# Three kinds of ScalarE work placed later in a planned order: a long convolution beside a feed-forward block

## The chip, the cores and the metric

The kernel runs on one core of one Trainium2 chip. The metric is the device time of one execution in microseconds, as the median of several runs. The core has five engines, each with a queue of its own that it works off in order: TensorE (PE in the profile) for matmuls, VectorE (DVE), ScalarE (ACT), GpSimd (POOL) and SyncE (SP). SP and POOL issue the transfers (DMAs) here. Engines wait for one another by semaphores.

## The reference

`x` has 2048 rows of 1024 columns. Two branches work on its layer norm, and their sum is added to `x`.

```
xn = layernorm(x)
k_shift = sum over 4 taps of k shifted by 0..3 rows, times shift_k      # short causal convolution
kv = k_shift * v
y  = irfft(rfft(kv padded to 4096) * rfft(ssm_k padded to 4096))[:2048] # long causal convolution
A  = xn * (y + kv * ssm_D)
B  = silu(xn @ w1) @ w2                                                # 1024 -> 3584 -> 1024
out = x + A + B
```

All inputs and the output are float32.

## The kernel before

**Two branches side by side.** The feed-forward part is two large matrix products (GEMM1 with `w1`, GEMM2 with `w2`) in fp16. Each float32 operand is split into a high part (ScalarE, a scaled copy) and a low part (VectorE, the remainder), and a product takes three matmuls: high by high, high by low, low by high. Most of it runs as Strassen products, seven (P1 to P7) in place of eight. Results leave PSUM by ScalarE copies and silus and by VectorE sums (`evacuate`, `silu`, `evacuate2`, `result`); there are four PSUM banks for it, the ring `ff`. Lines L980 to L982 are the three matmuls of GEMM1, L1123 to L1125 those of GEMM2.

The convolution works on eight groups of 128 channels (`g` from 0 to 7). For each group, `gate` makes the signal `acc` (the taps and the product with `v`, in the tile `sig`). `signal_parts` splits it into high and low parts and turns it, `stage1` transforms it by matmuls (L1625 to L1627, tile `ps`), and `to_spec`, `forward`, `product` and `inverse` do the rest of the transform on VectorE in the tile `spec`. `result_parts` splits the result (`zh`, `zl`), `stage1_inv` transforms it back (L1813 to L1815, tile `py`), and `gated` multiplies it by rows of `x` (tile `xg`, some in `ht`) and sends it to the output.

**The order of the work is planned when the program is built.** Every operation is an `Op` with an engine, an estimated duration and a `margin`. The generators above are streams that yield operations, and wait for flags and free buffers. `Order.prepare` reckons when the operands of a stream's next operation are there, by the planner's own clock, and adds the margin; for a transfer the clock assumes a fixed latency and 345 GB a second (in `Order.run`). `Order.run` then always takes the operation that could start first, less a small bias of its stream, puts it at the end of its engine's queue, and goes on. The chip works off each queue in exactly that order, however long its transfers really take. The usual margin of a ScalarE or VectorE operation is 0.15 us.

**The three places that the change touches.**

- *Squares of w2* (`squares_w2`, `square_w2`). The norm of `w2` is needed before `w2` can be split. 28 loads of 512 KB go in turn to two buffers, `wraw` and `w2n`; ScalarE squares each in place with a running total, and this frees the buffer for the next load. After the last one, `norms_w2` makes the scales (among them a small matmul, `py<-q,one`), and then loads `w2` a second time through the same two buffers to split it for GEMM2 (`x<-wraw,tau` and `x<-w2n,tau`). The stream's bias is 0.01, nearly the lowest.
- *Rows of x for the gate* (`norm_rows`, bias 0). For each group and each of four `t`, two transfers of 128 KB fill a tile of `xg` (four buffers; some tiles come from `ht`), and four ScalarE operations subtract the mean. A tile's successor in the stream is loaded after that. The tile is free again when `gated` has sent it out.
- *Parts of the conv signal* (`signal_parts`, first called for group 0 through TensorE, for the groups from 1 on through DMA). For each of four `t`, `split` writes the high and low part of a quarter of `acc` into the single buffer `cm`; two transposing DMAs (`X`, SP queue) carry them back into `acc` turned. The next quarter needs the buffer, and so the end of these DMAs.

In the profile nearly all ScalarE operations have line L362, those of VectorE L351 and L354, and transfers from SP L338, its transposing ones L344, since helpers issue them; they are told apart by the tiles they write and read.

Of the kernel before, what the change touches and what calls it, by code (L numbers as in the profile page):

```python
# [15 lines left out]
AF = mybir.ActivationFunctionType  # L16
# [103 lines left out]
class Order:  # L120
# [27 lines left out]
    def add(self, gen, bias, floor=0.0):  # L148
        s = Stream(gen, bias, floor)
        self.streams.append(s)  # L150
        self.advance(s)
# [151 lines left out]
def h3_ffn_kernel(ctx, tc, x, kp, vs, fs, shift, dskip, w1, w2, cfwd, cinv, out):  # L303
# [26 lines left out]
    def A(f, o, ins, us=None, m=0.15):  # L330
        return Op("ACT", us or 1.02 * (0.16 + size(o) * 0.84e-3), 0.2, f, ins, [o], m)

    def T(f, o, ins, us, m=0.1):
        return Op("PE", us, 0.3, f, ins, [o], m)

    def L(o, i, m=0.3):
        n = size(o) * o.shape[0] * mybir.dt.size(o.dtype)
        return Op("SP", 0.4, 0.1, lambda: nc.sync.dma_start(o, i), [i], [o], m, n)  # L338

    def X(o, i, m=0.3, k=None):  # L340

        n = size(o) * o.shape[0] * mybir.dt.size(o.dtype)
        k = k or (1.2 if i.space == bass.MemoryType.DRAM else 3.0)
        return Op("SP", 0.65 + n / 240e3, 0.1, lambda: nc.sync.dma_start(o, i, transpose=True), [i], [o], m, k * n)  # L344
# [8 lines left out]
    def v_stt(o, a, s, b, op0, op1, **k):  # L353
        return V(lambda: nc.vector.scalar_tensor_tensor(o, a, s, b, op0=op0, op1=op1), o,  # L354
                 [a, b] + ([] if isinstance(s, float) else [s]), **k)

    def a_act(o, i, func, scale=1.0, bias=None, total=None):
        def f():
            kw = {} if bias is None else {"bias": bias}
            if total is not None:  # L360
                kw["accum_out"] = total
            nc.scalar.activation(o, i, func, scale=scale, **kw)  # L362
        ins = [i] + [s for s in (scale, bias) if s is not None and not isinstance(s, float)]
        p = A(f, o, ins)
        p.table = func if func in (AF.Silu, AF.Sqrt) else None
        p.busy += 0.07 * (len(ins) - 1) - 0.06 * (i.space == bass.MemoryType.PSUM)
        if total is not None:
            p.busy += 0.19
            p.writes.append(total)
        return p  # L370

    def split(hi, lo, src, scale, after=()):

        yield a_act(hi, src, AF.Copy, scale)
        yield v_stt(lo, src, scale, hi, MUL, SUB)
        for t in after:
            t.set()
# [11 lines left out]
    mu = cst.tile([P, NT], F32, name="mu")  # L389
# [57 lines left out]
    def norm(ring, ss, ns, then, flags, margin=1.5):  # L447
# [27 lines left out]
        for t in flags[1]:  # L475
            t.set()


    def small(o, i, scale, ins=()):

        return Op("ACT", 0.2, 0.2, lambda: nc.scalar.activation(o, i, AF.Copy, scale=scale), [i, *ins], [o], 0.15)
# [110 lines left out]
    def turned(src, tok, name, i, bias):  # L592

        yield ft.ready
        pt, ptok = ft.tile([P, KH, P])

        def mm():
            for c in range(KH):
                nc.tensor.transpose(pt[:, c, :], src[:, c * P:(c + 1) * P], ident)
        yield T(mm, pt, [src], 0.44, m=0.3)  # L600
        flag["turned", name, i].set()
        if tok is not None:
            tok.set()
        o = factor(name)[:, i]
        after = (ptok, flag["x", 0, name]) + ((flag["rows", i],) if name in ("A11", "A12") else ())
        add(split(o[:, :, 0], o[:, :, 1], pt, XS, after), bias)
# [27 lines left out]
    def shipped(names, i, src, toks):  # L634

        def steps():
            yield xst_r.ready if len(names) == 1 else xst_r.pairs
            rows, rtok = (xst_r.tile if len(names) == 1 else xst_r.pair)([P, len(names) * KH, 2, P], F16, len(names))
            yield from split(rows[:, :, 0], rows[:, :, 1], src.rearrange("p (k w) -> p k w", w=P), XS, toks)
            for n, name in enumerate(names):  # L640
                add(across(name, i, rows[:, n * KH:(n + 1) * KH], rtok), URGENT.get(name, 0.1))
        add(steps(), URGENT.get(names[0], 0.1))
# [665 lines left out]
    def squares_w2():  # L1308

        yield lambda: "wraw" in ctxs  # L1310
        yield flag["unit", SQ]
        rings = ctxs["wraw"], ctxs["w2n"]
        for i in range(NP):
            for h in range(2):
                yield lambda: any(r.pairs() for r in rings)
                raw, tok = next(r for r in rings if r.pairs()).pair([P, 2, W])
                yield L(raw, w2r[:, 2 * i:2 * i + 2, h * W:(h + 1) * W])
                add(square_w2(raw, tok, ss2[:, i, h:h + 1]), 0.01)
# [1 line left out]
    flag["w2 squares"] = Token(2 * NP)  # L1320

    def square_w2(raw, tok, o):
        yield a_act(raw, raw, AF.Square, total=o)
        tok.set()
        flag["w2 squares"].set()

# [132 lines left out]
    def convolution(floor):  # L1459
# [9 lines left out]
        acc = sig[:, 0]  # L1469
# [17 lines left out]
        def rest(floor):  # L1487

            yield flag["w done"]
            yield flag["w spilled"]  # L1490
            early_w.close()
            rb = late_w.enter_context(tc.tile_pool(name="rb", bufs=1, side="right"))
            for name, bufs in (("zh", 2), ("zl", 2), ("xg", XGB)):
                more[name] = ring(name, bufs, rb)
            ctxs["wraw"] = Halves(order, rb, "wraw", 1)
            for gen, bias in ((result_parts(), CB), (stage1_inv(), 0.02), (norm_rows(), 0.0), (norms_w2(), 0.03)):
                add(gen, bias, max(order.free["DVE"], order.free["ACT"]))
# [68 lines left out]
        def signal_parts():  # L1566

            for g in range(NG):
                yield flag["scales", g]
                kf, ktok = kfs[g]  # L1570
                sc, _ = scs[g]
                whole = [kparts[:, :, q].rearrange("p b t w -> p b (t w)") for q in range(2)]
                add(split(*whole, kf.rearrange("p b t w -> p b (t w)"), sc[:, 1:2], (ktok, flag["kparts", g])), CB)
                for t in TO:
                    there = acc16.rearrange("p b (i t) w -> p (b i) t w", i=2)[:, :, t]
                    two = [there[:, :, q * P:(q + 1) * P] for q in range(2)]
                    if g < BY_DMA:
                        yield py_r.ready
                        px, ptok = py_r.tile([P, 2, 2, P])

                        def mm():
                            for b in range(2):
                                for i in range(2):
                                    nc.tensor.transpose(px[:, b, i, :], acc[:, b, t + 4 * i, :], ident)
                        yield T(mm, px, [acc[:, :, t::4, :]], 0.44, m=2.0)
                        add(split(*two, px.rearrange("p b i w -> p (b i) w"), sc[:, 0:1], (ptok, flag["part", g, t])), CB)
                        continue
                    yield cm_r.ready
                    cm, ctok = cm_r.tile([P, 2, 2, 2, P], F16, 2)
                    yield from split(cm[:, 0], cm[:, 1], acc[:, :, t::4, :], sc[:, 0:1])  # L1590
                    flag["part", g, t].n = 2
                    for q, o in enumerate(two):
                        yield X(o, cm[:, q].rearrange("p b i w -> p (b i w)"))
                        ctok.set()
                        flag["part", g, t].set()
# [188 lines left out]
        def norm_rows():  # L1784

            for g in range(NG):
                for t in TO:
                    r = more["xg"]
                    yield lambda: r.ready() or flag["quads", 1]() and hts.ready()
                    xgs[g, t] = xg, _ = (r if r.ready() else hts).tile([P, 2, 2, P], uses=2)  # L1790
                    for b in range(2):
                        yield L(xg[:, b], x4[b][:, :, t, g * P:(g + 1) * P])
                    for b in range(2):
                        for i in range(2):
                            n = b * T2 + 4 * i + t
                            yield a_act(xg[:, b, i], xg[:, b, i], AF.Identity, -1.0, mu[:, n:n + 1])
                    flag["xg", g, t].set()

        def stage1_inv():
# [48 lines left out]
        for gen, bias in ((loads(), 0.05), (load_v(), 0.04), (gate(), 0.04), (signal_parts(), CB), (stage1(), 0.02),  # L1848
                          (transforms(), 0.02), (squares_w2(), 0.0), (rest(floor), 0.0)):
            add(gen, bias, floor)  # L1850
# [113 lines left out]
```

## Time and profile before

| | us |
|---|---|
| median of 3 runs | 1244.58 (1244.14 to 1245.72) |
| the profiled execution, its own time | 1244.12 |
| its span, first to last instruction | 1242.0 |
| first and last GEMM1 matmul | 15.6, 578.2 |
| first and last GEMM2 matmul | 579.7, 1238.1 |

The busy share of the engines in 40 slices of 31 us, in tenths (9 is 90% or more):

```profile
PE   9999999999999999999999999999999999999998
...
DVE  7999996996999779998899799899989979997981
ACT  7868997886688897559752732753363374554351
...
DMA  9598989899799899879986558489576784888776
```

A row of a view of waits names the engine that waited, what it waited for, and the microseconds in total, the number of times and the longest. In a timeline each row has a start, a duration, the engine, the line, the operation, and the output, an arrow and the inputs; a bracket gives the idle time just ahead and who ended it. The end of a matmul is modelled, so consecutive ones overlap in the records.

### The profile page before, as it was taken

How to read it: one execution, taken by the hardware profiler on the slowest of the kernel's cores; microseconds unless marked ns; L12 is line 12 of the kernel's file. 1: busy time of each engine (PE TensorE's matmuls, PEld its weight loads, DVE VectorE, ACT ScalarE, POOL GpSimd, SP SyncE). 2: the span in 40 equal slices, each digit the busy share in tenths (PEclk: the TensorE clock that was granted, in tenths of full speed). 3: DMA queues.
4: the chain of work that ended last, by engine and by line, in shares of the span. 5: the costliest groups of instructions: out<-in, count | busy, mean ns of one | idle time of the engine just before them, and what ended most of it. 6: DMA issues, size and time to landing. Idle time of an engine off the chain costs nothing.

```text
span 1242.0 us, 16865 instructions
## 1 busy us (share of the span) xinstructions
PE 1227.1 (99%) x6044; PEld 596.2 (48%) x6044; DVE 1107.2 (89%) x1248; ACT 775.7 (62%) x1357; POOL 83.3 (7%) x93
## 2 busy tenths in 40 slices
PE   9999999999999999999999999999999999999998
PEld 8544444444444544445444544544444454444454
DVE  7999996996999779998899799899989979997981
ACT  7868997886688897559752732753363374554351
POOL 0000000000000000000000000001030130123123
PEclk9999999999999999999999999999999999999999
DMA  9598989899799899879986558489576784888776
GB/s 369 127 315 265 322 301 325 262 258 217 233 346 291 241 309 295 244 205 315 297 269 153 155 186 171 122 293 278 125 168 169 178 170 141 180 150 133 164 142 97
DMA packets 277700, 278.77 MB, mean 224 GB/s; under 512 B 85616, under 2 KB 204656, under 8 KB 276336
## 3 DMA queue, kind: packets, MB, share of 16 engines
q1 hardware_dynamic: 261888, 261.17, 70.2%
q0 software_dynamic: 15728, 16.52, 10.3%
q8 instruction: 47, 0.77, 0.3%
q14 instruction: 37, 0.30, 0.1%
HBM read 171.46 MB, written 88.34 MB: 209 GB/s over the span
## 4 chain that ended last, share of the span: by engine, by line
PE 70%; DVE 19%; DMA 4%; issue 3%; ACT 2%; SPq 0%; DVEq 0%; ACTq 0%
PE ff L980 10%; PE ff L981 10%; PE ff L982 10%; PE ff L1123 10%; PE ff L1124 10%; PE ff L1125 10%; DVE spec L351 7%; DVE tmp L351 2%; DVE wo L354 2%; DVE sig L354 1%; PE ps L1625 1%; PE ps L1627 1%; PE ps L1626 1%; DMA wraw<-in_w 1%; DVE x L354 1%
## 5 line engine op out<-in xcount | busy, mean ns | idle before, releaser
L1123 PE MATMUL ff<-x,wo 128*128 128x512 f16 x868 | 328.1, 378 | 2.0 <-ACT hf L362 0.9
L1125 PE MATMUL ff<-x,wo 128*128 128x512 f16 x868 | 328.1, 378 | 0.0
L1124 PE MATMUL ff<-x,wo 128*128 128x512 f16 x868 | 328.1, 378 | 0.0
L980 PE MATMUL ff<-x,wo 128*128 128x512 f16 (+1 forms) x808 | 302.8, 375 | 3.3 <-ACT hf L362 3.3
L982 PE MATMUL ff<-x,wo 128*128 128x512 f16 (+1 forms) x808 | 302.8, 375 | 0.0
L981 PE MATMUL ff<-x,wo 128*128 128x512 f16 (+1 forms) x808 | 302.8, 375 | 0.0
L351 DVE TENSOR_TENSOR spec<-spec 128x1024 f32<-128x1024 f32 (+2 forms) x232 | 259.3, 1146 | 2.0
L1125 PEld LDWEIGHTS <-wo 128*128 128x128 f16 x868 | 84.9, 98 | 101.6
L1124 PEld LDWEIGHTS <-wo 128*128 128x128 f16 x868 | 84.9, 98 | 101.3 <-issue 3.3
L1123 PEld LDWEIGHTS <-wo 128*128 128x128 f16 x868 | 85.8, 99 | 98.6
L982 PEld LDWEIGHTS <-wo 128*128 128x128 f16 x808 | 79.0, 98 | 92.4 <-DVE wo L354 0.5
L981 PEld LDWEIGHTS <-wo 128*128 128x128 f16 x808 | 79.0, 98 | 92.0 <-issue 3.9
L980 PEld LDWEIGHTS <-wo 128*128 128x128 f16 x808 | 80.5, 100 | 88.1
L351 DVE TENSOR_TENSOR tmp<-spec 128x2048 f32<-128x2048 f32 (+1 forms) x48 | 92.5, 1934 | 1.0
L354 DVE SCALAR_TENSOR_TENSOR ht<-hf,wsc,ht 128x1024 f16<-128x1024 f32 (+1 forms) x56 | 67.2, 1203 | 19.6 <-ACT ht L362 19.6
L362 ACT ACTIVATE spec<-spec 128x1024 bf16<-128x1024 f32 x32 | 33.7, 1053 | 59.6 <-DVE spec L351 59.5
L354 DVE SCALAR_TENSOR_TENSOR wo<-raw,wsc,wo 128x1024 f16<-128x1024 f32 (+1 forms) x56 | 63.9, 1147 | 4.4 <-ACT wo L362 4.0
L362 ACT ACTIVATE wo<-raw,wsc 128x1024 f16<-128x1024 f32 (+1 forms) x56 | 57.7, 1033 | 11.7 <-DVE raw L351 8.8
L354 DVE SCALAR_TENSOR_TENSOR sig<-kin,taps,sig 128x1024 f32<-128x1024 f32 x48 | 61.5, 1281 | 2.5 <-ACT sig L362 2.4
L348 POOL DMA_DIRECT2D out<-hf x44 | 39.3, 906 | 342.7 <-ACT hf L362 280.4
L351 DVE TENSOR_TENSOR spec<-tmp 128x512 f32<-128x512 f32 (+1 forms) x80 | 61.3, 794 | 1.1
L362 ACT ACTIVATE ht<-hf,wsc 128x1024 f16<-128x1024 f32 (+1 forms) x56 | 60.6, 1084 | 2.2 <-DVE hf L351 1.0
(191 smaller groups left out, 1695.3 us busy)
## 6 DMA issues: line engine op xcount, KB each, us to landing
wo<-hs SPq DMA_DIRECT2D x160, 256.0 KB, 3.6
hs<-ht SPq DMA_DIRECT2D x80, 256.0 KB, 4.7
raw<-in_w SPq DMA_DIRECT2D x28, 512.0 KB, 5.9
wraw<-in_w SPq DMA_DIRECT2D x24, 512.0 KB, 5.6
w2n<-in_w SPq DMA_DIRECT2D x24, 512.0 KB, 6.2
ws_T<-wo SPq DMA_DIRECT2D x22, 512.0 KB, 5.8
kin<-in_kp SPq DMA_DIRECT2D x16, 704.0 KB, 6.0
wo<-ws_T SPq DMA_DIRECT2D x22, 512.0 KB, 4.7
```

Of the source, the lines that this page charges most:

```text
L348: return Op("POOL", 1.1, 3.0, lambda: nc.gpsimd.dma_start(o, i, accum_op=ADD), [i], [o], m, 2.3 * n)
L351: return V(lambda: nc.vector.tensor_tensor(o, a, b, op=op), o, [a, b], **k)
L354: return V(lambda: nc.vector.scalar_tensor_tensor(o, a, s, b, op0=op0, op1=op1), o, [a, b] + ([] if isinstance(s, float) else [s]), **k)
L362: nc.scalar.activation(o, i, func, scale=scale, **kw)
L980: nc.tensor.matmul(o, w[:, 0, k], xf[:, :, k, 0], start=first and k == 0, stop=False, **kw)
L981: nc.tensor.matmul(o, w[:, 0, k], xf[:, :, k, 1], start=False, stop=False, **kw)
L982: nc.tensor.matmul(o, w[:, 1, k], xf[:, :, k, 0], start=False, stop=last and k == KH - 1, **kw)
L1123: nc.tensor.matmul(po, hx[:, n, 0, :], wc[:, n, 0, :], start=first and n == 0, stop=False, **kw)
L1124: nc.tensor.matmul(po, hx[:, n, 0, :], wc[:, n, 1, :], start=False, stop=False, **kw)
L1125: nc.tensor.matmul(po, hx[:, n, 1, :], wc[:, n, 0, :], start=False, stop=last and n == 3, **kw)
L1625: nc.tensor.matmul(o, cf[:, 0], h, start=i == 0, stop=False, **kw)
L1626: nc.tensor.matmul(o, cf[:, 0], l, start=False, stop=False, **kw)
```

## The change

A helper `later` raises the margin of one operation. The squares of w2 and the row operations of the gate get 4 us more, and the high part of a conv part 3 us more when it goes through `cm` (`split` has a new argument `wait` for it, 0 everywhere else). Nothing is added to or taken from the computation.

```diff
-    def split(hi, lo, src, scale, after=()):
+    def split(hi, lo, src, scale, after=(), wait=0.0):
 
-        yield a_act(hi, src, AF.Copy, scale)
+        yield later(a_act(hi, src, AF.Copy, scale), wait)
         yield v_stt(lo, src, scale, hi, MUL, SUB)
...
+    def later(op, us):
+
+        op.margin += us
+        return op
...
     def square_w2(raw, tok, o):
-        yield a_act(raw, raw, AF.Square, total=o)
+        yield later(a_act(raw, raw, AF.Square, total=o), 4)
         tok.set()
...
-                    yield from split(cm[:, 0], cm[:, 1], acc[:, :, t::4, :], sc[:, 0:1])
+                    yield from split(cm[:, 0], cm[:, 1], acc[:, :, t::4, :], sc[:, 0:1], wait=3)
...
-                            yield a_act(xg[:, b, i], xg[:, b, i], AF.Identity, -1.0, mu[:, n:n + 1])
+                            yield later(a_act(xg[:, b, i], xg[:, b, i], AF.Identity, -1.0, mu[:, n:n + 1]), 4)
```

## The prediction

> **What bounds the kernel now.** I read the page first: TensorE is busy nearly the whole span.
>
> ```profile
> PE 1227.1 (99%) x6044; PEld 596.2 (48%) x6044; DVE 1107.2 (89%) x1248; ACT 775.7 (62%) x1357; POOL 83.3 (7%) x93
> ```
>
> The busy times by stage say where the rest lies. Columns: the stage, its length, then busy time and count for PE, PEld, DVE, ACT and POOL, the granted clock, the DMA engines' busy share, GB/s.
>
> ```profile
> 62.00:310.00 248.00, 247.63 (x1171) 114.98 (x1170) 222.17 (x285) 197.28 (x300) 0.94 (x1) 1.00 0.93 283
> 330.00:355.00 25.00, 21.70 (x101) 9.69 (x99) 22.40 (x20) 17.42 (x31) 0.00 (x0) 1.00 0.78 262
> 355.00:1054.00 699.00, 697.49 (x3392) 332.23 (x3391) 643.82 (x654) 414.84 (x774) 33.63 (x35) 1.00 0.78 220
> 1054.00:1116.00 62.00, 60.27 (x291) 28.24 (x289) 59.32 (x68) 33.81 (x58) 8.66 (x10) 1.00 0.87 166
> ```
>
> From 62 to 310 us TensorE lacks 0.4 us, from 355 to 1054 it lacks 1.5, but 3.3 in the 25 us from 330 and 1.7 in the 62 from 1054. The clock is 1.00 throughout. So the change can win only what TensorE waits, and its waits name ScalarE (from 330 us on; total, times, longest):
>
> ```profile
> PE ff L980 <- ACT hf L362: 3.3, 2, 2.3
> PE py L1814 <- DVE zl L354: 1.7, 3, 1.1
> PE ff L1123 <- ACT hf L362: 0.9, 2, 0.5
> ...
> PE ff L1123 <- ACT ff L362: 0.4, 1, 0.4
> ```
>
> The timeline of ScalarE and then of TensorE shows the longest of them (start, duration, work; in brackets the idle time ahead and who ended it):
>
> ```profile
> 337.41 1.06 ACT L362 ACTIVATE wraw<-wraw 128x1024 f32<-128x1024 f32 x1 [5.74 <-DMA wraw<-in_w]
> ...
> 338.47 0.58 ACT L362 ACTIVATE ff<-ff 128x512 f32<-128x512 f32 x1
> 338.98 1.03 ACT L362 ACTIVATE w2n<-w2n 128x1024 f32<-128x1024 f32 x1
> ...
> 340.02 0.67 ACT L362 ACTIVATE hf<-ff,wsc 128x512 f32<-128x512 f32 x1
> ```
> ```profile
> 337.86 0.38 PE L981 MATMUL ff<-x,wo 128*128 128x512 f16 x1
> 338.07 0.38 PE L982 MATMUL ff<-x,wo 128*128 128x512 f16 x1
> 340.74 0.38 PE L980 MATMUL ff<-x,wo 128*128 128x512 f16 x1 [2.28 <-ACT hf L362]
> ```
>
> ScalarE stands 5.74 us before the first square of w2, whose rows have not landed. The silu of 340.02, which empties the PSUM bank TensorE wants next, stands behind this square and the next one. A second case is 13 us later: the square at 353.18 has 0.61 us of DMA wait, and the copy out of PSUM that follows it releases TensorE.
>
> ```profile
> 353.18 1.06 ACT L362 ACTIVATE wraw<-wraw 128x1024 f32<-128x1024 f32 x1 [0.61 <-DMA wraw<-in_w]
> 354.14 0.19 ACT L362 ACTIVATION_READ_ACCUMULATOR wraw<-wraw 128x1 f32 x1
> 354.24 0.58 ACT L362 ACTIVATE hf<-ff 128x512 f32<-128x512 f32 x1
> ```
> ```profile
> 354.86 0.38 PE L980 MATMUL ff<-x,wo 128*128 128x512 f16 x1 [1.02 <-ACT hf L362]
> ```
>
> In the stage from 1054 us it is a conv part: ScalarE waits for the transposing DMA that still reads the one `cm` buffer, and the evacuation behind it lets TensorE go on late.
>
> ```profile
> 1077.10 0.72 ACT L362 ACTIVATE cm<-sig,csc 128x512 f16<-128x512 f32 x1 [2.61 <-DMA sig<-cm]
> ...
> 1079.58 1.25 ACT L362 ACTIVATE hf<-ff,invc 128x512 f32<-128x512 f32 x2
> ```
> ```profile
> 1080.29 0.38 PE L1123 MATMUL ff<-x,wo 128*128 128x512 f16 x1 [0.41 <-ACT hf L362]
> ```
>
> ScalarE's waits of these kinds, over the whole kernel, sum to 61.4 us; nearly all of them cost TensorE nothing.
>
> ```profile
> ACT cm L362 <- DMA sig<-cm: 24.7, 11, 5.9
> ...
> ACT ht L362 <- DMA ht<-in_x: 15.8, 6, 5.6
> ...
> ACT xg L362 <- DMA xg<-in_x: 12.6, 4, 6.2
> ...
> ACT wraw L362 <- DMA wraw<-in_w: 8.3, 5, 5.7
> ```
>
> The Trainium skill ("Perfetto Trace Analysis", section "Identifying the Most-Contended Engine") judges TensorE by the busy share of its weight loads, not of its matmuls. By that rule 48% would leave about half the span, an estimated 640 us (52% of 1242), to be won. The trace differs: from 62 to 310 us, without waits, the share is 114.98 of 248 us, 46%, so 48% is full here.
>
> **The change part by part.** No instruction or transfer is added or removed. The planner gets a larger margin for three kinds of operation, so it starts them 3 or 4 us later in its own time, and other work of ScalarE comes first. Up to about 330 us none of them has come up, so the order there stays.
>
> *Squares of w2 (+4).* The two stalls at 340.74 and 354.86 go. A pause costs more than its idle time: matmuls start 0.21 us apart but last 0.38, so each pause hides another 0.16. Together 3.3 + 2 x 0.16 = 3.6 us, the first term. I take all of it: with both squares out of its way the silu needs only its own 0.67 us, if its product is done by then, which the row doesn't show; bounds 0 and 3.6.
>
> The price is that a square holds its buffer 4 us longer, and the next 512 KB load waits for it in SP's queue with everything behind it. The rows of the two buffers, of a load's landing (its last number), of the norm after the squares and of the first use of w2:
>
> ```profile
> L362 ACT ACTIVATE wraw<-wraw x14: 1040/1057/1066, 337.4 to 474.3; 128x1024 f32<-128x1024 f32 x14
> ```
> ```profile
> L362 ACT ACTIVATE w2n<-w2n x14: 1035/1043/1090, 339.0 to 480.7; 128x1024 f32<-128x1024 f32 x14
> ```
> ```profile
> wraw<-in_w SPq DMA_DIRECT2D x24, 512.0 KB, 5.6
> ```
> ```profile
> L457 PE MATMUL py<-q,one x2: 167/208/250, 485.5 to 485.5; 128*128 128x1 f32 x2
> ```
> ```profile
> L362 ACT ACTIVATE x<-wraw,tau x18: 706/1132/1157, 553.9 to 1071.4; 128x1024 f16<-128x1024 f32 x10, 128x512 f16<-128x512 f32 x8
> ```
> ```profile
> L1123 PE MATMUL ff<-x,wo x868: 269/379/380, 579.7 to 1237.9; 128*128 128x512 f16 x172, 128*128 128x256 f16 x2
> ```
>
> A buffer turns in (480.7 - 339.0)/13 = 10.9 us. With 14.9 us the last square starts at 339 + 4 + 13 x 14.9 = 537, the norm 4.8 later at 542, and the next load lands 5.6 us after that, at about 548. The first split of w2 is at 553.9, the first matmul on it at 579.7. So 56 us of delay end some 6 us before anyone asks: cost nothing.
>
> SP already waits for these squares, and everything behind their loads with it:
>
> ```profile
> SPq L338 <- ACT wraw L362: 10.3, 7, 3.8
> ```
>
> With the loads planned later too, this wait moves rather than grows; bounds -10.3 and +10.3 us of SP time, of which TensorE, released by ScalarE and not by a transfer in the rows above, feels nothing; I take 0.
>
> *Rows of x (+4).* Eight groups of four tiles, 128 operations. A tile's successor in the stream loads only after them, so up to 16 us per group.
>
> ```profile
> L362 ACT ACTIVATE xg<-xg,mu x80: 384/388/430, 341.8 to 1014.2; 128x128 f32<-128x128 f32 x80
> ...
> L351 DVE TENSOR_TENSOR xg<-py,xg x18: 682/685/693, 424.5 to 1203.9; 128x512 f32<-128x512 f32 x18
> ```
>
> First ready at 341.8, first multiplied at 424.5: 83 us of cover. Cost nothing; without cover, 16 us a group.
>
> *Conv parts (+3).* The first group goes through TensorE and keeps its order. In the other seven, four parts share one `cm` buffer in turn, so the fourth can come 12 us later, with its vector operation and its two transposing DMAs. Of the gaps to their matmuls the smallest I found is that of the group at 955 to 1010 us: the last DMA is issued at 984.26, lands 3.6 us later at 987.9, and the fourth part's matmul runs at 1005.2.
>
> ```profile
> 984.26 1.19 SPq L344 DMA_TRANSPOSE sig<-cm  x1
> ```
> ```profile
> L1625 PE MATMUL ff<-sig,cfw x2: 379/379/379, 1005.2 to 1008.4; 128*128 128x512 f16 x2
> ```
> ```profile
> sig<-cm SPq DMA_TRANSPOSE x56, 3.6
> ```
>
> 17.3 us against 12: hidden. The gain is in the stage from 1054 us: 0.9 + 0.4 idle and 3 x 0.16 make 1.8 us. I take half, 0.9, since the row at 1077.10 shows a DMA as the cause while other pauses have vector work ahead as well. Bounds 0 and 1.8.
>
> *A new order.* Everything behind the first moved operation is planned anew. What new pauses that makes no row shows. Nearest: TensorE lacks 1.5 us in the 699 us that the kernel's present order leaves alone. Bounds -1.7 (the pauses behind `zl` go as well) and, below, +11.4; I take half of 1.5, 0.75, as a loss.
>
> **Sum.** -3.6 - 0.9 + 0.75 = -3.75 us, on the profiled 1244.12 (span 1242.0 and 2.1 around it): 1240.4. The median of the runs lies 0.46 above that execution: **1240.8**.
>
> **The rivals.** *The gain is lost again* (22%): the pauses come back in other places, around 1244.0. For it: 61 us of waits cost only some 5, so which evacuation stands behind a late operation is chance. Against: the 5.74 us wait is the longest of its kind but for two.
>
> *The order hardly changes* (5%): the moved operations have almost the lowest priority and wait for a free ScalarE anyway; 1244.6. Against: ScalarE did idle 5.74 us before one. To this belongs the Trainium skill's rule that the memory side binds at some 358 GB/s ("DMA: Bandwidth & Descriptors", section "Where 436 GB/s comes from"): transfers late for lack of bandwidth would stay late. The trace has 262 GB/s at the stall and 283 where TensorE never waited, so it doesn't bear that out.
>
> *Slower* (20%): the delayed operations reach the head of ScalarE's queue just ahead of an evacuation. It decides once that evacuation is later than the 12 matmuls of a product cover, 12 x 0.215 = 2.6 us. Now 2 of 28 squares do this, 1.8 us each. The moved places are 28 squares, 32 groups of rows and 28 parts, 88; at one in fourteen 6.3 x 1.8 = 11.4 us; less the 4.5 won, 1251.5.
>
> *Squares too late for w2* (3%): if a turn grew by 8 us instead of 4, the last square would be at 593 and w2's first matmul some 30 us late: about 1270. It decides from some 6 us a turn.
>
> **Numbers.** The forecast has 50%, with its own range 1238.5 to 1242.1. The range goes from 1237.5 (all 1.8 us and the 1.7 behind `zl` won, no new pause) to 1251.5, where the slower case lies; what it leaves out is that case's further half and the late w2. A measurement of this kernel tells 0.2%, 2.5 us, from no change: below 1242.1 is faster (50%), above 1247.1 slower (20% + 3%), between them the rest (27%).
>
> **What would show it.** The stage from 330 to 355 us with TensorE busy over 24.5 us and no 5.74 us wait ahead of a square; the last square near 537, the first split of w2 still near 554; waits of `cm` and the rows for DMAs well below 61 us together; 1080 us without pauses. Wrong if TensorE's idle time from 355 to 1054 rises over 5 us, or if w2's first matmul waits for its split.

## The result and the profile after

The changed kernel takes 1239.77 us (median of 6 runs, 1238.82 to 1241.56) against 1244.53 us of the kernel before beside it; the ratio is 0.9959, with a 95% interval of 0.9944 to 0.9975. The forecast was 1240.8. The profiled execution took 1239.78 us, its span is 1237.8 us (before: 1242.0).

Busy times of the changed kernel in the stages that the prediction shows (same columns):

```profile
62.00:310.00 248.00, 247.63 (x1172) 114.99 (x1171) 222.21 (x285) 197.42 (x300) 0.94 (x1) 1.00 0.93 283
330.00:355.00 25.00, 25.00 (x117) 11.37 (x116) 25.00 (x22) 16.96 (x28) 0.00 (x0) 1.00 0.86 290
355.00:1054.00 699.00, 698.19 (x3395) 332.51 (x3394) 640.90 (x654) 418.41 (x782) 33.64 (x35) 1.00 0.78 220
1054.00:1116.00 62.00, 60.77 (x295) 28.75 (x294) 58.80 (x65) 29.22 (x50) 9.49 (x11) 1.00 0.79 171
```

The stage from 330 us is full now, with 117 matmuls where there were 101. The last two gained 0.7 and 0.5 us. TensorE's waits from 330 us on no longer have a row above 1.2 us:

```profile
PE ff L1128 <- ACT hf L362: 1.2, 1, 1.2
PE ff L1128 <- DVE hf L354: 0.6, 1, 0.6
PE ff L985 <- DVE hf L351: 0.5, 1, 0.5
PE ps L1630 <- DVE spec L351: 0.3, 1, 0.3
```

(The new helper shifts the lines by five: L985 to L987 and L1128 to L1130 are the matmuls of GEMM1 and GEMM2.) ScalarE's timeline shows what took the place of the 5.74 us wait:

```profile
333.28 0.58 ACT L362 ACTIVATE ff<-ff 128x512 f32<-128x512 f32 x1 [1.79 <-PE ff L987]
335.81 0.69 ACT L362 ACTIVATE hf<-ff,wsc 128x512 f32<-128x512 f32 x1 [1.95 <-PE ff L987]
336.53 1.15 ACT L362 ACTIVATE ht<-hf,wsc 128x1024 f16<-128x1024 f32 x1
337.59 1.04 ACT L362 ACTIVATE wraw<-wraw 128x1024 f32<-128x1024 f32 x1
```

The copy runs at 333.28 instead of 338.47, the silu at 335.81 instead of 340.02, each as soon as TensorE has its product. The square follows at 337.59, when its rows are there, and waits for nothing. Of the 61.4 us of waits for such transfers these are left, 6.6 us (a wait of 5.9 us for another kind, `out<-ht`, is new):

```profile
ACT xg L362 <- DMA xg<-in_x: 4.5, 2, 2.4
...
ACT cm L362 <- DMA sig<-cm: 2.1, 1, 2.1
```

The price shows where it was looked for. The rows of the second buffer, of the norm of w2, of the first split and of GEMM2's first matmul:

```profile
L362 ACT ACTIVATE w2n<-w2n x14: 1039/1048/1067, 338.6 to 518.9; 128x1024 f32<-128x1024 f32 x14
```
```profile
L457 PE MATMUL py<-q,one x2: 167/208/250, 523.3 to 523.3; 128*128 128x1 f32 x2
```
```profile
L362 ACT ACTIVATE x<-wraw,tau x18: 706/1132/1150, 551.0 to 1065.2; 128x1024 f16<-128x1024 f32 x10, 128x512 f16<-128x512 f32 x8
```
```profile
L1128 PE MATMUL ff<-x,wo x868: 270/379/379, 576.7 to 1232.4; 128*128 128x512 f16 x172, 128*128 128x256 f16 x2
```

The norm comes 38 us later than before, at 523.3, and yet the first split of w2 is 2.9 us earlier and GEMM2 starts 3.0 us earlier. SP's wait for the squares of one buffer, 10.3 us before, is 7.3 us:

```profile
SPq L338 <- ACT wraw L362: 7.3, 5, 3.3
```

### The profile page after: what moved, and what is told of

Same layout as the page of the kernel before. It is cut to its first block, busy times and chain, and to the rows that moved or that the text cites. A ratio compares the mean times of both kernels' runs of the same rounds, so it can differ in the third digit from the quotient of the medians.

```text
span 1237.8 us, 16864 instructions
## 1 busy us (share of the span) xinstructions
PE 1227.2 (99%) x6044; PEld 597.6 (48%) x6044; DVE 1106.9 (89%) x1248; ACT 775.0 (63%) x1357; POOL 83.3 (7%) x93
## 3 DMA queue, kind: packets, MB, share of 16 engines
q0 software_dynamic: 15728, 16.52, 10.3%
## 4 chain that ended last, share of the span: by engine, by line
PE 79%; DVE 15%; issue 3%; ACT 1%; DMA 1%; SPq 0%; DVEq 0%; ACTq 0%
PE ff L1128 13%; PE ff L1129 13%; PE ff L1130 13%; PE ff L985 9%; PE ff L986 9%; PE ff L987 9%; DVE spec L351 3%; DVE ht L354 2%; DVE x L354 2%; PE ps L1630 2%; PE ps L1631 2%; PE ps L1632 2%; DVE tmp L351 1%; DVE hf L351 1%; DVE wo L354 1%
## 5 line engine op out<-in xcount | busy, mean ns | idle before, releaser
L1128 PE MATMUL ff<-x,wo 128*128 128x512 f16 x868 | 328.1, 378 | 1.8 <-ACT hf L362 1.2
L1130 PE MATMUL ff<-x,wo 128*128 128x512 f16 x868 | 328.1, 378 | 0.0
L985 PE MATMUL ff<-x,wo 128*128 128x512 f16 (+1 forms) x808 | 302.7, 375 | 0.5 <-DVE hf L351 0.5
L987 PE MATMUL ff<-x,wo 128*128 128x512 f16 (+1 forms) x808 | 302.8, 375 | 0.0
L1130 PEld LDWEIGHTS <-wo 128*128 128x128 f16 x868 | 84.9, 98 | 101.6
L1128 PEld LDWEIGHTS <-wo 128*128 128x128 f16 x868 | 85.8, 99 | 99.0
L987 PEld LDWEIGHTS <-wo 128*128 128x128 f16 x808 | 79.0, 98 | 92.4 <-DVE wo L354 0.5
L985 PEld LDWEIGHTS <-wo 128*128 128x128 f16 x808 | 80.5, 100 | 88.2
```

The costliest lines, as they stand in the source:

```text
L985: nc.tensor.matmul(o, w[:, 0, k], xf[:, :, k, 0], start=first and k == 0, stop=False, **kw)
L987: nc.tensor.matmul(o, w[:, 1, k], xf[:, :, k, 0], start=False, stop=last and k == KH - 1, **kw)
L1128: nc.tensor.matmul(po, hx[:, n, 0, :], wc[:, n, 0, :], start=first and n == 0, stop=False, **kw)
L1130: nc.tensor.matmul(po, hx[:, n, 1, :], wc[:, n, 0, :], start=False, stop=last and n == 3, **kw)
```

## Experiments

A measure common to all: for each kernel's profile I took, from the start times of all matmuls, every interval between two starts less what the first of the two needs at full clock, and summed it by stage. The need is columns/2400 us and 0.0022 us, which is 0.2155 us for 512 columns and 0.109 us for 256, the distances of starts in stages without pauses. (Float32 columns count four times, a choice that moves a stage by some 0.1 us, as the float32 matmuls of these stages have 1 to 4 columns.) The sum is the time that TensorE lost, pauses and slow clock together. Some 1.6 us of the second column are no pause: in the kernel before, 26 of these small matmuls lie there, which start 0.07 us apart. Each row is one execution: the two rows of the changed kernel, of one and the same order, differ by up to 0.6 us.

| kernel | 330 to 360 | 360 to 1040 | 1040 to 1120 | against before, 95% interval |
|---|---|---|---|---|
| before | 3.7 | 4.5 | 2.9 | 1 |
| changed | 0.0 | 3.8 | 1.7 | 0.9959 [0.9944, 0.9975] |
| changed, second runs | 0.3 | 3.2 | 1.7 | 0.9967 [0.9952, 0.9981] |
| squares alone | 0.0 | 3.4 | 1.3 | 0.9957 [0.9942, 0.9972] |
| rows alone | 6.2 | 4.2 | 2.4 | 0.9999 [0.9986, 1.0011] |
| parts alone | 2.0 | 7.5 | 1.4 | 1.0006 [0.9995, 1.0016] |
| squares and rows | 0.4 | 4.6 | 0.4 | 0.9949 [0.9933, 0.9964] |
| squares and parts | 0.0 | 6.3 | 1.4 | 0.9975 [0.9966, 0.9983] |
| first square of each buffer | 0.2 | 4.4 | 1.4 | 0.9978 [0.9969, 0.9987] |
| all squares but these two | 2.0 | 4.6 | 2.2 | 0.9995 [0.9986, 1.0004] |
| squares by 2 us | 1.1 | 8.9 | 1.9 | 1.0014 [1.0001, 1.0027] |
| squares by 8 us | 0.0 | 32.2 | 1.8 | 1.0193 [1.0179, 1.0207] |
| squares by 12 us | 1.3 | 89.0 | 0.4 | 1.0660 [1.0646, 1.0675] |
| changed, and energies by 2 us | 1.4 | 3.8 | 0.4 | 0.9958 [0.9945, 0.9971] |

The ratios come from three groups of runs, four kernels each, in which the kernel before had medians of 1245.66, 1242.89 and 1244.99 us on its chip (the first line of the changed kernel apart). Within a group they compare directly; between groups the kernel before differs by up to 2.8 us, while the changed kernel took 1239.77 and 1240.39 us in its two sets of runs.

**One kind at a time.** The margins of the other kinds are set to 0.

```diff
-        yield later(a_act(raw, raw, AF.Square, total=o), 4)     # squares
+        yield later(a_act(raw, raw, AF.Square, total=o), 0)
-                            ... mu[:, n:n + 1]), 4)             # rows
+                            ... mu[:, n:n + 1]), 0)
-                    ... sc[:, 0:1], wait=3)                     # parts
+                    ... sc[:, 0:1], wait=0.0)
```

> Only the squares of w2 get the 4 us; rows and parts stay. Theory (each kind takes away its own waits): the two pauses at 338 and 353 us go, 3.6 us, and the rest of the order is as good or bad as any other: 1241.0, with ScalarE's waits for the cm buffer and for rows near the 24.7 and 28.4 us of before. Rival (what matters is that everything is planned anew): the gain doesn't follow the squares, between 1240 and 1248.

> Only the row operations of the gate get 4 us. Theory: their waits of 28.4 us shrink to under 8, but the pauses at 338 and 353 us belong to the squares and stay: 1244.5, within 1.5. Rival (planned anew): anything from 1240 to 1248; if the pause at 338 goes here too, the theory is wrong.

> Only the conv parts get 3 us. The first moved part comes at about 372 us, so up to there the queues are those of before and both early pauses stay. Theory: the stage from 1040 to 1120 us wins 1 to 2 us: 1243.3; ScalarE's waits for cm fall from 24.7 us to under 6. Rival: between 1240 and 1248, and the stage from 1054 unchanged or worse.

> Squares and rows get 4 us, parts none. Theory: as the squares alone, 1241.0, since the rows had 83 us of cover. Rival: more than 1.5 us away from the squares alone on either side.

Measured: 1239.54, 1246.04, 1246.63 and 1239.13 us, with 1245.66 for the kernel before. The squares alone win all that the whole change wins; rows alone and parts alone win nothing that can be told from noise. The stage from 330 us says why. With the squares alone it is full:

```profile
330.00:355.00 25.00, 25.00 (x118) 11.29 (x117) 25.00 (x23) 17.11 (x28) 0.00 (x0) 1.00 0.83 279
```

With the parts alone it lacks 1.7 us, as nothing has moved there yet; the parts' own waits did shrink, from 24.7 us to 7.8 (I had said under 6). The stage from 1040 us did win the 1 to 2 us of the theory (2.9 lost before, 1.4 now), but from 360 to 1040 us this order loses 3.0 us more, and nothing is left for the time:

```profile
330.00:355.00 25.00, 23.29 (x108) 10.45 (x107) 22.79 (x20) 18.10 (x32) 0.00 (x0) 1.00 0.79 268
```
```profile
ACT cm L362 <- DMA sig<-cm: 7.8, 3, 3.4
```

The rows alone had their waits gone too (no row for `ht<-in_x` is left, and 4.6 us for `xg`), with the same time. What TensorE's clock did in this run stands at the end. The rows came out 1.5 us above the theory's 1244.5, on a chip where the kernel before took 1.1 us more than in the first runs; the parts missed theirs, 1243.3, by 3.3 us.

These runs also show how much the early pause varies by itself. ScalarE's order is that of the kernel before up to 378 us with the parts alone, and up to the silu behind the squares with the rows alone, and the waits from 330 to 360 us are these, first of the parts alone and then of the rows alone:

```profile
PE ff L985 <- ACT hf L362: 1.7, 1, 1.7
```
```profile
PE ff L985 <- ACT hf L362: 3.1, 1, 3.1
```

In the profile of the kernel before they were 3.3 us in two pauses. The second pause, of 1.02 us at 353, did not come with the parts alone, though nothing had moved ahead of it. So the pause belongs to the order, but its size belongs to the execution: what is lost from 330 to 360 us is 3.7 us in the one profile of the kernel before, 2.0 with the parts alone and 6.2 with the rows alone.

**The first square, and the others.** The square's margin becomes an argument:

```diff
-                add(square_w2(raw, tok, ss2[:, i, h:h + 1]), 0.01)
+                add(square_w2(raw, tok, ss2[:, i, h:h + 1], 4 if i == 0 else 0), 0.01)   # first pair; 0 if i == 0 else 4: the others
```

> Only the very first square in each of the two buffers gets 4 us; the other 26 squares, the rows and the parts stay. Theory (the gain is one place: the first square, whose load leaves late, holds up the silu behind it): the pauses of 330 to 360 us go and nearly the whole gain of the squares alone comes, 1240 to 1241.5. Rival (many squares each give a little): under a third of it, above 1243.

> The other 26 squares get 4 us, the first of each buffer none. Theory: the wait of some 5.7 us ahead of the first square and TensorE's pause near 338 us stay: 1244 to 1246. Rival: most of the gain of the squares alone, below 1242.5.

Measured: 1239.74 and 1241.86 us; the kernel before 1242.89. Two margins of the 28 give 0.9978, the other 26 give 0.9995, whose interval holds 1. The same stage, first with the first pair moved and then with all but the first pair:

```profile
330.00:355.00 25.00, 24.98 (x117) 11.22 (x116) 25.00 (x21) 16.14 (x26) 0.00 (x0) 1.00 0.83 284
```
```profile
330.00:355.00 25.00, 23.16 (x109) 10.40 (x107) 22.59 (x20) 17.13 (x31) 0.00 (x0) 1.00 0.77 260
```

In the second, ScalarE's timeline is that of before, 1.3 us later:

```profile
338.69 1.06 ACT L362 ACTIVATE wraw<-wraw 128x1024 f32<-128x1024 f32 x1 [5.66 <-DMA wraw<-in_w]
...
341.30 0.66 ACT L362 ACTIVATE hf<-ff,wsc 128x512 f32<-128x512 f32 x1
```

So the sure part of the gain is one place: the two squares that come first. How much of the gain it is remains open. The first pair wins 3.2 us against the kernel before on its chip, the squares alone 6.1 us on theirs, and the two were not run side by side; by the time lost in the three stages the pair saves 5.1 us and all squares 6.4 us. Not all expectations held. The pair came out at 1239.74, just under the 1240 to 1241.5 that I had. The other 26 came out at 1241.86 where I had 1244 to 1246, and so below the 1242.5 that I had set for the rival, mostly since the kernel before ran faster on this chip as well, by 2.8 us than in the group ahead; only the ratio, 0.9995, speaks against the rival.

**More margin, and less.** Only the squares move, by 8, 12 and 2 us.

```diff
-        yield later(a_act(raw, raw, AF.Square, total=o), 4)
+        yield later(a_act(raw, raw, AF.Square, total=o), 8)
```

> Squares alone, 8 us in place of 4. My working of the buffers' turn (10.9 us and 8 more) puts the last square near 593 and w2's first matmul some 28 us late: about 1268. If a turn grows by less than the margin, as with 4 us, where it grew by about 3, the last square is at about 579 and the matmul 10 to 15 us late, 1250 to 1255, unless the planner puts other work of TensorE in the gap.

> Squares alone, 12 us. Ring of buffers as the limit: 13 turns of 21 to 23 us, last square between 620 and 650, w2's first matmul 45 to 85 us late, 1285 to 1325, less what convolution work fills. Rival (the ring never limits, w2's norm has room): within 3 us of the squares by 4.

> Squares alone by 2 us. In the kernel before, the first square went ahead of a copy and a silu whose inputs TensorE had ready some 2 and 4.5 us after ScalarE fell idle at 331.7. Theory: 2 us pass the copy at least, the silu perhaps not; so the pause of 330 to 360 us is gone or under 2.5 us: 1239.5 to 1242. Rival (any margin reshuffles to the same gain): as the squares by 4, within 0.7.

Measured: 1266.84, 1325.01 and 1246.76 us. With 8 us the ring of two buffers is the limit, as the prediction worked out for its fourth rival: the last square at 592.1 (the working says 593) and GEMM2's first matmul at 605.8.

```profile
L362 ACT ACTIVATE w2n<-w2n x14: 1040/1043/1066, 347.8 to 592.1; 128x1024 f32<-128x1024 f32 x14
```
```profile
PE ff L1128 <- ACT x L362: 10.6, 1, 10.6
PE py L457 <- DVE q L1340: 8.4, 1, 8.4
PE ff L1129 <- DVE x L354: 3.5, 3, 2.2
```

TensorE waits 8.4 us for the sums of the squares, then 10.6 us for the first split of w2. With 12 us the last square is at 647.6, between 620 and 650 as expected, and the time is at the upper end of what I had, 1285 to 1325. I had left room for work of the convolution in the gap, but TensorE's longest wait is for that work itself, ahead of a small matmul for its scales:

```profile
PE py L497 <- ACT sig L362: 32.6, 2, 28.0
PE py L457 <- DVE q L1340: 20.8, 1, 20.8
```

Moving the squares is thus worth 6 us at 4 us of margin (1245.66 to 1239.54) and costs 24 at 8 (1242.89 to 1266.84) and 82 at 12 (to 1325.01), each against the kernel before on its chip.

With 2 us the copy passes the first square and the silu doesn't:

```profile
334.55 0.58 ACT L362 ACTIVATE ff<-ff 128x512 f32<-128x512 f32 x1 [1.52 <-PE ff L987]
338.78 1.06 ACT L362 ACTIVATE wraw<-wraw 128x1024 f32<-128x1024 f32 x1 [3.64 <-DMA wraw<-in_w]
...
339.83 0.67 ACT L362 ACTIVATE hf<-ff,wsc 128x512 f32<-128x512 f32 x1
```

The stage from 330 us loses 1.1 us, inside the bound I gave, but the time, 1246.76, misses both theories: from 360 to 1040 us this order loses 8.9 us where the one of before loses 4.5. So a margin that cures the early pause in the main (1.1 us lost where it was 3.7) need not win anything.

**Parts on top of squares, energies on top of all.** The last adds a margin for the square sums that follow VectorE's product:

```diff
-            yield a_act(j.bitcast(BF16), o, AF.Square, 2.0 ** -48, total=s)
+            yield later(a_act(j.bitcast(BF16), o, AF.Square, 2.0 ** -48, total=s), 2)
```

> The changed kernel once more, on the chip of the three others, as their measure: 1239.8, and what the two chips so far leave open is whether the gain here is nearer 3 or nearer 6 us; by the theory that the pause near 338 us now and then takes the clock down with it, it is large where the kernel before shows granted clocks under 0.999.

> Squares by 4 us and parts by 3, rows none. Theory: the parts are worth nothing by themselves, so as the squares alone, 0.996 of before within 0.0015. Rival (the parts win 1 to 2 us in the stage from 1040 to 1120 once the early pauses are gone): 0.9945 or less.

> The changed kernel, and the square sums of the spectra (energy), which make ScalarE wait 65.9 us for VectorE, get 2 us more as well. Theory: the one pause over 1 us that is left behind 360 us, at 1086, stands behind such a wait and goes: 1.4 us less than the changed kernel on the same chip. Rival (waits ahead of an evacuation cost nothing where VectorE is the limit, and a new order brings its own pauses): within 1 us of it on either side.

Measured: 1240.39, 1241.51 and 1239.62 us, the kernel before 1244.99. In the last kernel a sum that comes later can read a spectrum that the inverse transform has begun to overwrite, so the scales of the convolution are other ones; instructions and sizes are the same, but it no longer computes the reference, and its time speaks of the order alone. (That the sum reads an overwritten spectrum follows from the program's text, where the inverse transform doesn't wait for it; no trace shows it.) The changed kernel has its longest remaining pause, 1.2 us, behind such a sum:

```profile
1084.72 1.06 ACT L362 ACTIVATE spec<-spec 128x1024 bf16<-128x1024 f32 x1 [3.96 <-DVE spec L351]
1085.68 0.19 ACT L362 ACTIVATION_READ_ACCUMULATOR spec<-spec 128x1 f32 x1
1085.78 0.67 ACT L362 ACTIVATE hf<-ff,invc 128x512 f32<-128x512 f32 x1
```

With the energies moved the stage from 1054 to 1116 us is full, and 1.4 us come back elsewhere, from 330 to 360: the ratios, 0.9958 and 0.9967, don't tell the two apart. That is what the rival said (within 1 us); the theory's 1.4 us did not come. Squares and parts lose, from 360 to 1040, 2.9 us more than the squares alone, and their ratios, though from two groups and with intervals that touch, lie apart the same way. No version here is measurably better than the changed kernel.

## Why the prediction was right, step by step

- *Squares, 3.6 us won.* The mechanism was right: the copy and the silu went ahead of the squares, and 3.7 us lost there became 0.0. The assumption in it, that the silu's product was ready, held: it was done by 335.8. That the size fits is in part luck, as it is taken from one execution, and other executions of the same order up to there lost 2.0 and 6.2 us.
- *Squares, their price nothing.* Right, with room to spare. A turn of a buffer grew from 10.9 to 13.9 us, not to 14.9: the last square came at 518.9 instead of 537. Why it grew by less than the margin no run shows; with 8 and 12 us it grew by about the whole margin (7.9 and 12.2 us). The point from which it would decide, some 6 us a turn, is between the 4 and the 8 us that ran.
- *Rows, nothing.* Right: 0.9999 alone.
- *Parts, hidden, and 0.9 us won.* Hidden they were in the group that I worked out (its last transposing DMA is issued at 987.63 us, 3.4 us later than before, and no matmul waits for it), but the gain isn't theirs. The stage from 1040 us lost 2.9 us before and 1.7 now, about the amount forecast; without any margin on the parts, squares alone and squares with rows lose 1.3 and 0.4 there. This step put a pause down to the wait that stood ahead of it, when several other new orders of that stage were as good a cure (not all: with the rows alone it still lost 2.4).
- *A new order, 0.75 us lost.* The sign was wrong, if by little: from 360 to 1040 us the changed kernel loses 0.7 us less than the one before, 1.3 less in its second profile. The kernels in the table whose margins are 4 us or less lie between 3.2 and 8.9, before at 4.5, so this term is worth -1.3 to +4.4 us; nothing in the rows of before told where in this range a new order would fall.
- *Not in the sum:* what comes after the last matmul took 1.3 us more in the changed kernel's profile (it starts at 1232.6 of 1237.8 us, before at 1238.1 of 1242.0). The start of the last matmul moved by 5.5 us, the span by 4.2. In its second profile it took 0.6 us more than before.
- *The sum.* The forecast was -3.75 us, and the span moved by -4.2. The closeness is partly luck: the three stages of the table won 5.6 us where the sum had 3.75, most of the difference in the term for the new order, and the end took back 1.3 us that no term had.
- *The signs.* Met: the stage from 330 us is full, the first split of w2 is at 551.0, the waits for DMAs are 6.6 us, and from 355 to 1054 us TensorE lacks 0.8 us, under the 5 that would have been wrong. Missed: the last square at 518.9 instead of 537, and the stage around 1080 us, which kept a pause of 1.2 us.
- *The rivals.* Lost again: it did not happen to the changed kernel, and it did to the squares by 2 us. Hardly any other order: no, the copy and the silu passed the square. Slower by 88 moved places: with 88 places moved, no pause behind 360 us lost more than 1.4 us. Squares too late: not at 4 us; at 8 it costs about what it said (1266.84 us, said 1270). (In the passage on what bounds the kernel, 52% of 1242 us is 646, not 640; nothing hangs on it.)

## What to carry to other kernels

In an order fixed beforehand, a wait for a transfer costs only what stands behind it in the same queue: of 61 us of such waits here one of 5.7 us cost most, since a silu that frees a PSUM bank stood behind it. Look for the bound engine's pause first and follow it back to that one operation; the margin of two operations there is the part of the gain that these runs make sure of. Allow for what the new order does elsewhere, which no row foretold here: with the squares by 2 us it lost 4.4 us where the early pause gave back 2.6. Work out beforehand how far the buffers that the late operation holds can be stretched, since the loss beyond that was four times the gain at 8 us and thirteen times at 12.

## What the runs showed of the hardware

The clock of TensorE can fall after a single pause. With the rows alone the pause near 338 us was 3.12 us, and after it the matmuls of 512 columns start 0.43 us apart and no longer 0.22:

```profile
338.57 0.38 PE L987 MATMUL ff<-x,wo 128*128 128x512 f16 x1
342.07 0.59 PE L985 MATMUL ff<-x,wo 128*128 128x512 f16 x1 [3.12 <-ACT hf L362]
342.45 0.64 PE L986 MATMUL ff<-x,wo 128*128 128x512 f16 x1
342.88 0.63 PE L987 MATMUL ff<-x,wo 128*128 128x512 f16 x1
```

The granted clock, the third number from the end of a row, is at 1.00 again in the row from 350 us:

```profile
335.00:340.00 5.00, 3.95 (x19) 1.67 (x18) 5.00 (x5) 1.25 (x3) 0.00 (x0) 1.00 0.75 251
340.00:345.00 5.00, 2.93 (x7) 1.02 (x7) 3.66 (x5) 4.25 (x8) 0.00 (x0) 0.61 0.78 252
345.00:350.00 5.00, 5.00 (x18) 2.03 (x17) 4.40 (x3) 3.30 (x5) 0.00 (x0) 0.71 0.99 345
350.00:355.00 5.00, 5.00 (x25) 2.27 (x24) 3.82 (x4) 4.31 (x7) 0.00 (x0) 1.00 1.05 346
```

So a pause of 3.3 us beyond the pace (342.07 - 338.57 - 0.22) cost 6.2 us in the end. In the profile of the kernel before, the same place had 2.28 us of idle time and kept its clock:

```profile
340.00:345.00 5.00, 4.26 (x20) 1.95 (x20) 3.64 (x3) 4.97 (x11) 0.00 (x0) 1.00 0.97 314
```

The Trainium skill ("TensorE: Matmul & The Clock Gate", section "Part 1: The HAM clock gate (the "warmup" mystery)") says that the array runs at half clock after an idle window of about 3.4 us and at full clock after about as long a busy one. The trace agrees in kind but not in size: 3.12 us of idle time were enough, and the matmuls stayed slow from 342.07 to 347.97 us, 5.9 us.

The kernel before spreads from 1241.5 to 1249.1 us on one chip, with mean granted clocks from 0.997 to 1.000. This pause, when it is long enough to halve the clock, may be a part of that: with the rows alone, where it halved the clock, ScalarE's order up to the silu is that of the kernel before. Of the executions of the kernel before on that chip the seven at 1.000 took 1243.9 us in the mean, the two at 0.997 1248.7. It can't be all, as the seven alone lie between 1241.5 and 1246.4 us. There is no trace of a long execution of the kernel before, so this stays open.
